# Reading DRAM in 32 KB runs that land in two partitions each, in a single-query attention kernel

## The chip, the cores and the metric

The kernel runs on one core of a Trainium2 chip. The metric is the device time of one execution in microseconds (us), as a median over several runs.

## The reference, cut to what matters

Two decode-attention blocks with one query each, their results side by side:

```python
# A: 32 heads, 32 key/value heads, 32,768 keys of 128 elements, bf16
q = (x @ wq).reshape(32, 128)
p = softmax(q @ k_cache.T * 128 ** -0.5)      # per head
a = (p @ v_cache).reshape(4096) @ wo
# B: the same with 8 key/value heads (4 query heads share one) and the last 4096 keys alone
out = concatenate([a, b])
```

Block A's keys and values are 2 x 32 x 32768 x 128 x 2 bytes = 512 MiB (537 MB). Everything else (block B's keys and values, the projection weights) brings the traffic to 570 MB. Each key and each value is used once, so the kernel streams.

## The kernel before: the parts that matter

Keys of A come in units of 2 MB: one head, 8192 keys. Partition p holds 64 consecutive keys, 16 KB in a row in DRAM and 16 KB in a row on the chip. A value buffer holds two heads and is filled by two such loads. All loads are issued by SyncE in program order; each waits until the buffer that it fills has been read.

```python
class _Kernel:
    NK = 4      # key buffers of 16 KB per partition
    NV = 3      # value buffers of 32 KB per partition
    ...
    def kv_src(self, name, which, h0, nh, r):
        d = self.X[name]
        base = d["key0"] + d["blk"] * r                 # blk: 8192 keys in A
        ap = d[which][0, h0:h0 + nh, base:base + d["blk"], :]
        return ap.rearrange("s (p j) d -> p s (j d)", p=128)

    def load(self, dst, src, sem, *deps):
        self.op("sp", lambda e: e.dma_start(dst, src).then_inc(sem, 16), *deps)
    ...
    # load_k: one head of A (two of B) into one key buffer
        dst = self.kbuf[slot][:, :].rearrange("p (s x) -> p s x", s=d["kpu"])
        self.load(dst, self.kv_src(name, "k", h0, d["kpu"], r), self.ksem[slot], ...)
    # load_v: one half of a value buffer
        dst = self.vbuf[slot][:, half * w:(half + 1) * w].rearrange("p (s x) -> p s x", s=nh)
        self.load(dst, self.kv_src(name, "v", h0, nh, r), self.vsem[slot][half], ...)
```

After landing, TensorE transposes the keys in 128 x 128 tiles, VectorE copies the transposes out, TensorE multiplies them with the query; softmax statistics are kept over rounds of 8 heads x 8192 keys, and the value products of one round run beside the key work of the next.

## Time and profile before

1366.77 us, median of 3 runs (1366.75 to 1367.38).

| what | value | how to read it |
|---|---|---|
| bytes read | 570 MB | at the rate of the next line they take 1338 us |
| rate from 120 to 1300 us | 426 GB/s | from the table by stretches, nearly flat over 40 slices |
| share of the DMA engines in that time | 1.01 | by the DMA records 16 or more packets are at work in 99% of that time |
| TensorE, VectorE busy in that time | 71%, 57% | both are idle for part of it |
| DMA in the chain that ended last | 77% | the kernel waits for data |

These are lines of the page of the kernel before: span, the DMA rows of the 40 slices, packets and bytes, the two large DMA queues (packets, MB, share of the 16 engines' span) and the shares of the chain that ended last.

```profile
span 1365.0 us, 32343 instructions
DMA  9999999999999999999999999999999999999995
GB/s 392 422 425 426 427 426 427 427 425 427 425 426 427 426 426 427 425 426 427 427 424 427 425 427 427 425 426 426 427 426 425 426 426 428 426 426 425 426 405 213
DMA packets 40762, 572.51 MB, mean 419 GB/s; under 512 B 4659, under 2 KB 4661, under 8 KB 4789
q1 hardware_dynamic: 40340, 570.44, 98.5%
q8 instruction: 119, 1.95, 0.6%
DMA 77%; PE 20%; DVE 1%; issue 1%; SPq 0%; ACT 0%
```

The table by stretches of the same kernel (start:end, length, busy time and instructions of each engine, TensorE's granted clock, DMA share, GB/s):

```profile
core 0: us, PE busy (x) PEld busy (x) DVE busy (x) ACT busy (x) POOL busy (x), PEclk, DMA share, GB/s
120.00:1300.00 1180.00, 833.00 (x13381) 650.75 (x13382) 674.30 (x1188) 23.07 (x59) 0.00 (x0) 0.85 1.01 426
1300.00:1330.00 30.00, 11.18 (x229) 7.05 (x226) 8.35 (x30) 1.74 (x5) 0.00 (x0) 0.77 0.95 401
```

The DMA queue's own waits (SyncE's) are for buffers to come free, which is what a queue that runs ahead looks like (block A's loads land 33.8 and 38.4 us after their issue, medians for keys and values). A line gives the waiting engine and its line, what released it (psS holds scores, psT transposed keys), us in total, times, and the longest wait:

```profile
SPq L203 <- PE psS L444: 1033.2, 115, 13.4
SPq L203 <- PE psT L417: 128.4, 12, 14.6
```

So the only thing worth changing for most of the span is how fast the 16 engines move bytes. The trace also has every DMA packet with its duration. From those records: 16 KB packets take 611 ns at best and 616.4 ns on average from 120 to 1300 us, while packets of 4, 8 and 12 KB take about 159, 309 and 460 ns at best. A line of 36.8 ns per 1000 bytes plus 8.5 ns per packet runs through these (a packet of "16 KB" has 16,384 bytes). Its slope gives an estimate of the ceiling: 27.2 GB/s for an engine, 435 GB/s for the 16 of the page, less a fixed cost of 1.4% at 16 KB (8.5 of 611 ns).

### The profile page before, as it was taken

What the parts mean: (1) busy time and instruction counts of PE and PEld (TensorE: products, weight loads), DVE (VectorE), ACT (ScalarE), POOL (GpSimd) and SP (SyncE); (2) the same over time, 40 slices, a digit from 0 to 9 for tenths busy, and PEclk for the clock granted to TensorE, in tenths of its full rate; (3) what the DMA queues carried; (4) which work ended last, traced back from release to release, by engine and by line L of the source; (5) the groups of instructions that cost most, each with busy time, mean ns of one, the idle gap of its engine ahead of it and who ended that gap; (6) DMA issues with size and microseconds to landing.
All of it is one profiled execution on the core that took longest, in us unless ns stands there. A gap on an engine that the chain in (4) does not pass through costs nothing.

```text
span 1365.0 us, 32343 instructions
## 1 busy us (share of the span) xinstructions
PE 951.6 (70%) x15172; PEld 734.7 (54%) x15172; DVE 767.8 (56%) x1414; ACT 29.9 (2%) x73; POOL 2.4 (0%) x11
## 2 busy tenths in 40 slices
PE   5689766776777687676667767766766767687646
PEld 4466555655555465555556545555655545465423
DVE  4688555655656555564655646555565656555431
ACT  0000000000000000000000000000000000000000
POOL 0000000000000000000000000000000000000000
PEclk9889878878988887887888888878888898887877
DMA  9999999999999999999999999999999999999995
GB/s 392 422 425 426 427 426 427 427 425 427 425 426 427 426 426 427 425 426 427 427 424 427 425 427 427 425 426 426 427 426 425 426 426 428 426 426 425 426 405 213
DMA packets 40762, 572.51 MB, mean 419 GB/s; under 512 B 4659, under 2 KB 4661, under 8 KB 4789
## 3 DMA queue, kind: packets, MB, share of 16 engines
q1 hardware_dynamic: 40340, 570.44, 98.5%
q8 instruction: 119, 1.95, 0.6%
q14 instruction: 15, 0.11, 0.0%
q10 hardware_dynamic: 288, 0.00, 0.0%
HBM read 570.43 MB, written 0.00 MB: 418 GB/s over the span
## 4 chain that ended last, share of the span: by engine, by line
DMA 77%; PE 20%; DVE 1%; issue 1%; SPq 0%; ACT 0%
DMA kbuf<-in_A_k_cache_dram 73%; PE psT L417 15%; PE psS L444 3%; DMA kbuf<-in_B_k_cache_dram 3%; DMA vbuf<-in_A_v_cache_dram 2%; PE psS L583 1%; PE psACC L525 1%; DVE kt L421 0%; SPq L203 0%; DVE oc_B L551 0%; PE psPT L565 0%; ACT psb L472 0%; DVE o_B L535 0%; DVE tr_in L460 0%; DVE nbg_B L491 0%
## 5 line engine op out<-in xcount | busy, mean ns | idle before, releaser
L421 DVE COPY kt<-psT 128x1024 bf16<-128x1024 bf16 x1056 | 672.5, 685 | 427.0 <-PE psT L417 423.7
L417 PE MATMUL psT<-ident,kbuf 128*128 128x128 bf16 x8448 | 641.3, 243 | 361.2 <-DMA kbuf<-in_A_k_cache_dram 294.9
L417 PEld LDWEIGHTS psT<-ident,kbuf 128*128 128x128 bf16 x8448 | 577.5, 111 | 489.8 <-DMA kbuf<-in_A_k_cache_dram 335.6
L444 PE MATMUL psS<-kt,qz_A 128*32 128x512 bf16 x2048 | 177.2, 427 | 0.0
L525 PE MATMUL psACC<-vbuf,ptsb 128*8 128x256 bf16 (+1 forms) x4160 | 132.9, 283 | 23.9 <-issue 21.7
L525 PEld LDWEIGHTS psACC<-vbuf,ptsb 128*8 128x8 bf16 (+1 forms) x4160 | 103.0, 89 | 55.2 <-issue 23.4
L537 DVE SCALAR_TENSOR_TENSOR o_A<-o_A,alpha_A,psACC 128x256 f32<-128x256 f32 x48 | 23.1, 480 | 87.5 <-PE psACC L525 87.5
L444 PEld LDWEIGHTS psS<-kt,qz_A 128*32 128x32 bf16 x2048 | 32.1, 97 | 31.5 <-issue 10.4
L472 ACT ACTIVATE psb<-psS,nb_A 128x512 bf16<-128x512 f32 x16 | 11.0, 687 | 1157.8 <-DVE nb_A L470 1157.8
L535 DVE COPY o_A<-psACC 128x256 f32<-128x256 f32 x16 | 6.8, 424 | 19.9 <-PE psACC L525 19.9
L503 PEld LDWEIGHTS psPT<-ident,psb 128*128 128x128 bf16 x72 | 5.7, 123 | 15.3 <-issue 11.8
L503 PE MATMUL psPT<-ident,psb 128*128 128x128 bf16 x72 | 10.2, 290 | 2.9 <-ACT psb L472 2.9
L460 DVE TENSOR_REDUCE tr_in<-psS 128x1 f32<-128x512 f32 x18 | 12.2, 680 | 0.0
L507 ACT ACTIVATE ptsb<-psPT 128x512 bf16<-128x512 bf16 x18 | 10.7, 596 | 52.8 <-PE psPT L503 52.8
L395 PE MATMUL psACC<-x_B,vbuf 128*128 128x1 bf16 x128 | 3.7, 165 | 11.5 <-DMA x_B<-in_B_x_dram 10.9
L551 DVE SCALAR_TENSOR_TENSOR oc_A<-o_A,gmask_A,oc_A 128x128 f32<-128x128 f32 x28 | 9.9, 352 | 1.0
L395 PEld LDWEIGHTS psACC<-x_B,vbuf 128*128 128x128 bf16 x128 | 3.6, 104 | 11.6 <-DMA x_B<-in_B_x_dram 10.9
L479 DVE SCALAR_TENSOR_TENSOR l_A<-l_A,alpha_A,rs_A 128x1 f32<-128x1 f32 x12 | 2.6, 220 | 12.3 <-ACT alpha_A L477 12.3
L588 DVE CAST out_sb<-psS 1x512 bf16<-1x512 f32 x2 | 1.4, 678 | 14.1 <-PE psS L583 14.1
L583 PE MATMUL psS<-kbuf,oz_A 128*1 128x512 bf16 x32 | 8.3, 422 | 0.6 <-DVE oz_A L572 0.6
L583 PE MATMUL psS<-kbuf,oz_B 128*1 128x512 bf16 x32 | 7.1, 379 | 0.0
L583 PEld LDWEIGHTS psS<-kbuf,oz_A 128*1 128x1 bf16 x32 | 2.8, 90 | 5.6 <-issue 2.4
(72 smaller groups left out, 83.4 us busy)
## 6 DMA issues: line engine op xcount, KB each, us to landing
kbuf<-in_A_k_cache_dram SPq DMA_DIRECT2D x128, 2048.0 KB, 33.8
vbuf<-in_A_v_cache_dram SPq DMA_DIRECT2D x128, 2048.0 KB, 38.4
kbuf<-in_B_k_cache_dram SPq DMA_DIRECT2D x4, 2048.0 KB, 28.8
vbuf<-in_B_v_cache_dram SPq DMA_DIRECT2D x4, 2048.0 KB, 37.4
vbuf<-in_B_wq_dram SPq DMA_DIRECT2D x2, 2048.0 KB, 9.8
vbuf<-in_A_wq_dram SPq DMA_DIRECT2D x2, 2048.0 KB, 28.6
kbuf<-in_B_wo_dram SPq DMA_DIRECT2D x2, 2048.0 KB, 36.9
kbuf<-in_A_wo_dram SPq DMA_DIRECT2D x1, 2048.0 KB, 38.8
```

The costliest lines, as they stand in the source:

```text
L395: inst = e.matmul(ps[:, h:h + 1], lhsT=wq[:, 4096 * tt + 128 * h:4096 * tt + 128 * h + 128], rhs=t["x"][:, tt:tt + 1], start=(tt == 0 and ...
L417: inst = e.transpose(T[:, 128 * k:128 * k + 128], self.kbuf[slot][:, DH * tile:DH * tile + DH], self.ident[:, :])
L421: self.tcopy.append(self.op("dve", lambda v, T=T, KT=KT: v.tensor_copy(KT[:, :], T[:, :]), o, self.sread.get(b - self.NKT)))
L444: inst = e.matmul(bank[32 * c:32 * c + 32, :], lhsT=t["qz"][:, off:off + 32], rhs=self.kt[(b0 + c // 2) % self.NKT][:, 512 * (c % 2):512 * ...
L460: o = dve(lambda v: v.reduce_max(tr["in"][:, 0:1], self.S[i % 2][:, :], axis=AXX), sdone)
L472: e = self.op("act", lambda s: s.activation(out=pb[:, :], in_=self.S[i % 2][:, :], func=ACTF.Exp, bias=t["nb"][:, r:r + 1], scale=self.SCA ...
L503: inst = e.transpose(PT[:, 128 * jj:128 * jj + 128], pb[:, 128 * jj:128 * jj + 128], self.ident[:, :])
L507: "act", lambda s: s.activation(out=pt[:, :], in_=PT[:, 0:512], func=ACTF.Copy), o, self.pvlast.get(i - 2))
L525: inst = e.matmul(acc[32 * c:32 * c + HG, 0:w], lhsT=pt[:, col:col + HG], rhs=vv[:, :, 16 * kc + 4 * c + jj, :], start=(kc == 0 and jj == ...
L537: ou = self.op("dve", lambda v: v.scalar_tensor_tensor(out=t["o"][:, osl], in0=t["o"][:, osl], scalar=t["alpha"][:, r:r + 1], in1=acc[:, 0:w],
L551: prev = self.op("dve", lambda v, src=src, gm=gm: v.scalar_tensor_tensor(out=t["oc"][:, :], in0=src, scalar=gm, in1=t["oc"][:, :], op0=ALU ...
L583: inst = e.matmul(bank[0:1, 0:512], lhsT=t["oz"][:, a:a + 1], rhs=self.wo_at(name, a), start=(a == 0), stop=(a == 31), skip_group_check=True)
```

## The change

The intent: a larger run in DRAM, so half as many read pieces and, if the fixed cost is theirs, half of it. In DRAM partition p's 16 KB are followed directly by partition p+1's. One read of 32 KB can therefore supply two partitions. On the chip the two parts are in different partitions, so the writes stay 16 KB.

```diff
+    RUN = 16384                       # elements of 2 bytes
...
+    def load_wide(self, dst, src, sem, *deps):
+        def go(e):
+            pin, pout = (... for x in (e.lower_ap_dma(src), e.lower_ap_dma(dst)))
+            total = ...               # product of the sizes in pin.ap
+            pin = copy.replace(pin, ap=[[self.RUN, total // self.RUN], [1, 1], [1, self.RUN]])
+            pout = copy.replace(pout, ap=[list(pout.ap[0]), [1, 1], list(pout.ap[-1])])
+            e.add_instruction(mybir.InstDMACopy(..., mode="Copy", ins=[pin], outs=[pout],
+                queue="qSPDynamicHW", cce_op=ALU.bypass)).then_inc(sem, 16)
+        self.op("sp", go, *deps)
...
-        self.load(dst, self.kv_src(name, "k", h0, d["kpu"], r), ...)
+        (self.load_wide if d["kpu"] == 1 else self.load)(dst, self.kv_src(name, "k", h0, d["kpu"], r), ...)
...
-        self.load(dst, self.kv_src(name, "v", h0, nh, r), ...)
+        (self.load_wide if nh == 1 else self.load)(dst, self.kv_src(name, "v", h0, nh, r), ...)
```

The source of a load becomes 64 x 32 KB, the destination stays 128 x 16 KB. Only block A's 256 loads are concerned.

More of the change, by code (lines that the diff above doesn't have):

```diff
@@ L1 @@
+import copy
 import concourse.bass as bass
@@ L203, in load @@
         self.op("sp", lambda e: e.dma_start(dst, src).then_inc(sem, 16), *deps)
+    def load_wide(self, dst, src, sem, *deps):
+        def go(e):
+            pin, pout = (x[0] if isinstance(x, (list, tuple)) else x for x in (e.lower_ap_dma(src), e.lower_ap_dma(dst)))
+            total = 1
+            for _, n in pin.ap:
+                total *= n
+            pin = copy.replace(pin, ap=[[self.RUN, total // self.RUN], [1, 1], [1, self.RUN]])
+            pout = copy.replace(pout, ap=[list(pout.ap[0]), [1, 1], list(pout.ap[-1])])
+            e.add_instruction(mybir.InstDMACopy(
+                name=f"I-{self.nc.next_id()}", engine=mybir.EngineType.SP, mode="Copy", ins=[pin], outs=[pout],
+                queue="qSPDynamicHW", cce_op=ALU.bypass)).then_inc(sem, 16)
+        self.op("sp", go, *deps)
     def load_k(self, i, u):
@@ L213, in load_k @@
         dst = self.kbuf[slot][:, :].rearrange("p (s x) -> p s x", s=d["kpu"])
-        self.load(dst, self.kv_src(name, "k", h0, d["kpu"], r), self.ksem[slot], self.kfree[n - self.NK] if n >= self.NK else None)
+        (self.load_wide if d["kpu"] == 1 else self.load)(dst, self.kv_src(name, "k", h0, d["kpu"], r), self.ksem[slot], self.kfree[n - self.NK] if n >= self.NK else None)
         self.kwhere[(i, u)] = (n, slot, (self.ksem[slot], 16 * (fill + 1)))
@@ L231, in load_v @@
         dst = self.vbuf[slot][:, half * w:(half + 1) * w].rearrange("p (s x) -> p s x", s=nh)
-        self.load(dst, self.kv_src(name, "v", h0, nh, r), self.vsem[slot][half], self.vfree[n - self.NV] if n >= self.NV else None)
+        (self.load_wide if nh == 1 else self.load)(dst, self.kv_src(name, "v", h0, nh, r), self.vsem[slot][half], self.vfree[n - self.NV] if n >= self.NV else None)
     def load_wq(self, name):
```

## The prediction

> **What bounds the kernel.** The DMA engines. The page's utilisation rows show them at nine tenths or more in 39 of 40 slices, moving 425 to 427 GB/s; the table by stretches gives 426 GB/s and a DMA share of 1.01 from 120 to 1300 us, with TensorE busy 71% and VectorE 57%. The chain that ended last is 77% DMA, nearly all key loads. SyncE's own waits (1033 us on the score matmuls) are for free buffers; loads are issued 34 to 38 us before landing, some seven 2 MB loads deep, so the engines don't run dry before the tail, which the change doesn't touch.
>
> **What the change does.** 128 key and 128 value loads of block A (512 MiB of the 570 MB) keep their bytes, 16 KB writes, semaphores and order. Each reads 64 runs of 32 KB where it read 128 of 16 KB. Block B's loads and the weights stay. No compute instruction changes.
>
> **Cost per packet.** The trace's DMA records give for 4, 8, 12 and 16 KB packets about 159, 309, 460 and 611 ns at their fastest: 36.8 ns per KB (27.2 GB/s for one engine, 435 for 16) plus some 8.5 ns per packet.[...] The mean 16 KB packet takes 616.7 ns: 98% of that ceiling. Removing every fixed cost of A's loads would save (616.7-602.4) x 8 x 256 = 29 us, an upper bound just at 2%.
>
> **What it saves.** One engine has 8 packets per load. If the 8.5 ns belong to the read side, halving the reads saves 4 x 8.5 = 34 ns per load and engine, 256 loads: 8.7 us, all on the critical path, as DMA bounds every stage of A. If they belong to the write side, nothing is saved. If some of the further 5.6 ns of jitter per packet also comes from switching reads, up to 3 us more. I weigh the first case a little over the second: about 7 us saved.
>
> **Risks.** The two sides now have different shapes (64 against 128 entries).[...] I take this as one in twelve. A gain over 2% would need more than the ceiling.
>
> **What the profile would show.** If right: A's records become 32 KB of 1213 to 1222 ns if counted by reads (packets fall by about 16,400 from 40,762), the steady rate rises from 426 to about 429 GB/s, bytes and number of loads stay, the chain stays three quarters DMA, TensorE and VectorE stay near 952 and 768 us busy. If 32 KB takes exactly twice 611 ns, the fixed cost is the write side's and the time is unchanged.[...] If the rate rises but the time doesn't fall, TensorE limits in places (its granted clock is 0.85), which I don't expect.
>
> **What would make it wrong.** The fixed cost sits wholly on writes (no gain); uneven engines[...] (a loss); or a rate above 27.2 GB/s per engine that no packet here shows (a larger gain).
>
> Predicted 1359.5 us, range 1346 to 1368.5; faster by over 2%: 0.07, within 2%: 0.86, slower by over 2%: 0.07.

8.7 us for the read side, up to 3 us more and nothing for the write side were weighed to about 7 us off 1366.8, predicted as 1359.5. "That ceiling" is the 435 GB/s of the line above.

## The result and the profile after

1366.98 us (1365.66 to 1367.39, 4 runs) against 1367.08 us (1366.75 to 1370.0, 4 runs) of the kernel before in the same rounds. The ratio is 0.9993, with a 95% interval of 0.9976 to 1.001. A ratio here is the mean time of one kernel's fast runs over the mean time of the other's fast runs of the same rounds, so it is not quite the ratio of the two medians. A second measurement (below) gave 1.0003 (0.999 to 1.0015). The change does nothing to the time.

The same lines of the page of the changed kernel:

```profile
span 1363.9 us, 32343 instructions
DMA  9999999999999999999999999999999999999995
GB/s 393 422 423 425 428 426 425 426 429 428 423 425 427 428 425 426 427 429 426 425 423 429 427 426 425 425 429 424 425 426 427 428 426 426 426 427 425 425 409 223
DMA packets 24378, 572.51 MB, mean 420 GB/s; under 512 B 4659, under 2 KB 4661, under 8 KB 4789
q1 hardware_dynamic: 23956, 570.44, 98.4%
q8 instruction: 119, 1.95, 0.6%
DMA 77%; PE 20%; DVE 1%; issue 1%; SPq 0%; ACT 0%
```

Its table by stretches and the queue's own waits:

```profile
core 0: us, PE busy (x) PEld busy (x) DVE busy (x) ACT busy (x) POOL busy (x), PEclk, DMA share, GB/s
120.00:1300.00 1180.00, 826.41 (x13394) 646.79 (x13394) 674.27 (x1190) 23.19 (x59) 0.00 (x0) 0.86 1.00 426
1300.00:1330.00 30.00, 10.15 (x215) 6.32 (x212) 7.52 (x29) 1.74 (x5) 0.00 (x0) 0.69 0.97 409
```

```profile
SPq L217 <- PE psS L461: 1018.2, 117, 18.6
SPq L217 <- PE psT L434: 125.0, 11, 14.2
```

What the reader should see: the reads did become larger, as the packets fell from 40,762 to 24,378, exactly 16,384 fewer (256 loads x 64). A record is thus one read piece. Yet the steady rate is 426 GB/s before and after. The DMA share fell from 1.01 to 1.00 without any byte arriving sooner: the records of consecutive packets overlap by a few ns, and fewer records overlap less often (an estimate from e3 below, where records of 89 ns on average give a share of 1.05: about 4 ns each). So the sum of packet durations is not a throughput at this precision; the GB/s row is.

The duration of a 32 KB record tells why. From 120 to 1300 us its median is 1227 ns, which is twice the 614 ns median of a 16 KB record (1228). One fixed cost of 8.5 ns less would have made it about 1219 (an estimate from the line above).

### The profile page after: what moved, and what is told of

The parts are those of the page before. It is cut to its first block, busy times and chain, and to the rows that moved or that the text cites. A ratio compares the mean times of both kernels' runs of the same rounds, so it can differ in the third digit from the quotient of the medians.

```text
span 1363.9 us, 32343 instructions
## 1 busy us (share of the span) xinstructions
PE 944.6 (69%) x15172; PEld 730.4 (54%) x15172; DVE 767.1 (56%) x1414; ACT 29.9 (2%) x73; POOL 2.4 (0%) x11
## 2 busy tenths in 40 slices
DMA packets 24378, 572.51 MB, mean 420 GB/s; under 512 B 4659, under 2 KB 4661, under 8 KB 4789
## 3 DMA queue, kind: packets, MB, share of 16 engines
q8 instruction: 119, 1.95, 0.6%
## 4 chain that ended last, share of the span: by engine, by line
DMA 77%; PE 20%; DVE 1%; issue 1%; SPq 0%; ACT 0%
DMA kbuf<-in_A_k_cache_dram 73%; PE psT L434 15%; PE psS L461 3%; DMA kbuf<-in_B_k_cache_dram 3%; DMA vbuf<-in_A_v_cache_dram 2%; PE psS L600 1%; PE psACC L542 1%; DVE kt L438 0%; SPq L206 0%; DVE oc_B L568 0%; PE psPT L582 0%; ACT psb L489 0%; DVE o_B L552 0%; DVE tr_in L477 0%; DVE nbg_B L508 0%
```

## The experiments

Theory W: the fixed cost is paid for each write piece, and reads are free at these sizes. Theory R: it is paid for each read piece and the saving was lost elsewhere. Theory C, a form of R: the loads could go faster, but TensorE and VectorE give the buffers back too late.

In the first three experiments only the two access patterns of A's loads change. Written as (run of the read, run of the write):

```diff
-  pin  ap=[[16384, 64], [1, 1], [1, 16384]]      # the changed kernel: reads of 32 KB
-  pout ap=[pout.ap[0], [1, 1], [1, 8192]]        #                     writes of 16 KB
+  pin  ap=[[8192, 128], [8192, 1], [1, 8192]]    # e1: reads of 16 KB; e3: [1024, 8], [1, 1024] inside
+  pout ap=[pout.ap[0], [1024, 8], [1, 1024]]     # e1, e2 and e3: eight writes of 2 KB side by side
```

The opposite pair (small reads, one large write), which would test the read side most directly, is not among the runs.

### e1: reads of 16 KB, writes of 2 KB

> Block A's loads read 16 KB runs as before, but every 16 KB write is split into eight writes of 2 KB (same bytes, same place). Theory W (about 8.5 ns are paid per write piece): 16 KB of one engine takes 602 + 8 x 8.5 = 670 ns in place of 611, so 59.5 ns x 8 x 256 = 122 us more, about 1489 us, and some 390 GB/s in steady state. Theory R (paid per read piece, the time of the changed kernel held up by something else): no change, 1367 us.

Measured: 1494.79 us, one look, against 1367.31 us before. That is 127.5 us more. With a load's 128 packets spread evenly over 16 engines, one engine writes 56 more pieces per load, 14,336 in 256 loads: 127.5 us / 14,336 = 8.9 ns per piece (an estimate). (The 9.4 ns in the expectations of e5 come from the steady rates, 385 against 426 GB/s, and not from the whole time.) The state of a single look is unknown, but the trace puts the loss in the packets: from 120 to 1300 us the median 16 KB record takes 681 ns in place of 614.

### e2: reads of 32 KB, writes of 2 KB

> Reads of 32 KB, writes of 2 KB. Theory W: the same as with 16 KB reads and 2 KB writes, about 1489 us, as the reads count for nothing. Theory R: 1358 to 1367 us. If reads and writes each add their own cost: about 9 us below the run with 16 KB reads.

Measured: 1496.77 us, one look. Half as many reads as in e1, and no gain.

### e3: reads of 2 KB, writes of 2 KB

> Reads of 2 KB and writes of 2 KB. Theory W: still about 1489 us, although there are eight times as many reads as with 16 KB reads. Theory R: this one alone of the three is slow, about 1489 us. If both sides add: about 1611 us.

Measured: 1496.23 us, one look. Eight times the reads of e1, sixteen times those of e2, and the same time within 0.13% over all three. The tables by stretches of e1, e2 and e3, in this order, show the same rate:

```profile
120.00:1300.00 1180.00, 779.67 (x12178) 611.78 (x12171) 619.26 (x1094) 21.95 (x55) 0.00 (x0) 0.84 1.01 385
```

```profile
120.00:1300.00 1180.00, 776.63 (x12154) 609.33 (x12156) 617.20 (x1089) 21.96 (x55) 0.00 (x0) 0.84 1.00 385
```

```profile
120.00:1300.00 1180.00, 784.96 (x12158) 614.78 (x12158) 618.46 (x1089) 21.95 (x55) 0.00 (x0) 0.83 1.05 385
```

And their packet lines, e1, e2, e3: reads per kernel differ by more than ten times, the rate does not.

```profile
DMA packets 40761, 572.51 MB, mean 383 GB/s; under 512 B 4658, under 2 KB 4660, under 8 KB 4788
```

```profile
DMA packets 24377, 572.51 MB, mean 383 GB/s; under 512 B 4658, under 2 KB 4660, under 8 KB 4788
```

```profile
DMA packets 270137, 572.51 MB, mean 383 GB/s; under 512 B 4658, under 2 KB 4660, under 8 KB 266932
```

Theory R falls. It also falls that both sides add (e3 would have been near 1611 us). Theory W foretold all three within 0.6%.

### e4: half of the key compute left out

```diff
-                for k in range(8):        # transposes of a batch
+                for k in range(4):
-  v.tensor_copy(KT[:, :], T[:, :])
+  v.tensor_copy(KT[:, 0:512], T[:, 0:512])
   # and the score matmuls read columns 0:512 twice
```

> The changed kernel with half of the key transposes and half of the copy of each batch left out (a wrong result on purpose), all loads as they are. Theory C (TensorE and VectorE give buffers back too late, and so ate a gain of the loads): the time falls clearly below 1358 us. Theory W: the loads alone set the time, so it stays within about 5 us of 1367 us (the last stretch after the last keys may get a little shorter), and the steady rate stays at 426 GB/s.

Measured: 1359.67 us (1359.57 to 1360.64, 4 runs), ratio 0.9946 (0.9929 to 0.9962) to the kernel before. That is 7.6 us less, more than the 5 us that I had allowed, yet not the time clearly below 1358 us that theory C asked for. The stretches of this run:

```profile
120.00:1300.00 1180.00, 687.54 (x9635) 449.25 (x9634) 445.29 (x1200) 23.09 (x59) 0.00 (x0) 0.76 1.00 427
1300.00:1330.00 30.00, 9.90 (x181) 6.10 (x184) 2.92 (x11) 0.78 (x2) 0.00 (x0) 0.61 1.00 426
```

VectorE's busy time of the main stretch fell by a third (674 to 445 us), and the rate rose only from 426 to 427 GB/s; the 32 KB record kept its 1227 ns median. More is at the end: from 1300 to 1330 us the rate is 426 GB/s in place of 409, so the compute holds up the last loads a little. Part of the rise in the main stretch may come from the instruction stream, which the page counts on the same 16 DMA engines (0.4% of their span in place of 0.6%): 33 fewer instruction packets (86 in place of 119), 0.54 MB, 1.3 us at 426 GB/s over the whole run (an estimate). I did not separate these parts further. The control, the kernel before with half of its key compute, was not run, so the 7.6 us alone do not refute theory C. What speaks against it is the packets: with the compute halved, a 32 KB record still takes 1227 ns, twice 614, so there is no gain of the reads that late buffers could have eaten.

### e5, e6, e7: fewer write pieces, with controls

If W holds, the way to a gain is a larger write. I took 32 KB in a row in one partition on both sides, and for that regrouped block A: a round is now 4 heads x 16,384 keys in place of 8 heads x 8192, so a partition holds 128 keys of one head (32 KB). A load is 4 MB, and two key buffers lie side by side. The core of the edit:

```diff
-        a["KC"], b["KC"] = 4, 2                        # 8 heads, 8192 keys a round
+        a["KC"], b["KC"] = 8, 2                        # 4 heads, 16384 keys a round
+    RUN_R = 16384     # e5 and e6; 8192 in e7          # elements of a read
+    RUN_W = 16384     # e5; 8192 in e6 and e7          # elements of a write
+            pin  = copy.replace(pin,  ap=[[16384, 128], [R, 16384 // R], [1, R]])
+            pout = copy.replace(pout, ap=[pout.ap[0],   [W, 16384 // W], [1, W]])
...          # units address half a head; value buffers hold one head; two groups of 4 heads
...          # share the last matmuls of a group, so that results start at partitions 0, 32, 64, 96
```

These three kernels differ in nothing but the two run lengths.

> Block A regrouped, the result still right: a round takes 4 heads and 16,384 keys in place of 8 heads and 8192 keys, so one partition's keys and values of a load are 32 KB in a row on both sides, and a load is 4 MB. Reads 32 KB, writes 32 KB. Theory W, with 9.4 ns per write piece as the runs with 2 KB writes gave: one write piece less for every 32 KB, 4.7 ns per 16 KB and engine, so 4.7 x 8 x 256 = 9.7 us below the same kernel with 16 KB writes, some 430 GB/s in place of 426 to 427. It runs about 4,000 more value matmuls, which cost a little instruction traffic, so against the kernel before about 1357 to 1364 us. If only narrow writes cost extra and 16 KB is already free of it: the same time as with 16 KB writes.

> The regrouped kernel with 32 KB reads, each landing as two 16 KB writes: the control for the write size. Theory W: about 1367 to 1374 us, 9.7 us above the one with 32 KB writes. A rival by which the size of the load or the regrouping makes any gain: equal to the one with 32 KB writes.

> The regrouped kernel with 16 KB reads and 16 KB writes: the studied change, undone in this form. Theory W: equal to the one with 32 KB reads and 16 KB writes within 2 us. Theory R: 9 to 10 us slower than it.

| kernel | read, write | us, median (runs) | ratio to before |
|---|---|---|---|
| e5 | 32 KB, 32 KB | 1369.69 (6) | 1.0019 (1.0007 to 1.0032) |
| e6 | 32 KB, 16 KB | 1379.70 (5) | 1.0086 (1.0073 to 1.0099) |
| e7 | 16 KB, 16 KB | 1380.54 (4) | 1.0094 (1.0081 to 1.0107) |

The write size is worth 10.0 us in the medians and 9.4 us in the means (1379.3 less 1369.9); 9.7 was expected. One engine writes 1024 pieces fewer (by the same even spread), so a piece costs 9.2 ns by the means. The steady rates of e6 and e7, in this order, are to be held against e5's 426 GB/s further below:

```profile
160.00:1250.00 1090.00, 765.53 (x15740) 613.77 (x15744) 619.77 (x1149) 21.98 (x55) 0.00 (x0) 0.85 1.00 423
160.00:1250.00 1090.00, 762.55 (x15744) 611.27 (x15744) 618.86 (x1148) 21.98 (x55) 0.00 (x0) 0.85 1.00 423
```

The read size (e7 against e6, which is the studied change in this form) is worth 0.8 us in the medians, with overlapping intervals. The 32 KB record shows the worth of the write size directly: its median from 120 to 1300 us is 1227 ns when it lands as two writes (e6) and 1214 ns when it lands as one (e5).

But the regrouping lost more than the write size won. The stretches of e5:

```profile
80.00:120.00 40.00, 34.55 (x518) 26.23 (x515) 31.73 (x54) 0.00 (x0) 0.00 (x0) 0.91 0.86 355
160.00:1250.00 1090.00, 763.31 (x15956) 611.70 (x15953) 623.45 (x1158) 22.59 (x56) 0.00 (x0) 0.85 1.00 426
```

From 80 to 120 us the DMA moved 355 GB/s: with two 4 MB key buffers, the next key load waits for a whole buffer (from 60 to 130 us SyncE waited four times for score matmuls, 63.4 us in all and up to 23.8), and the value loads stand behind it in SyncE's order. Shorter dips, to between 408 and 421 GB/s in single slices of the page, came back through the run.

### e8, e9: three key buffers and two value buffers

```diff
-    NK = 4        # key buffers of 16 KB a partition, used in pairs; lines that place the output weights are left out
-    NV = 3        # value buffers of 32 KB a partition
+    NK = 6
+    NV = 2
```

> The regrouped kernel with 32 KB reads and writes lost what it gained: between 80 and 120 us it moved 355 GB/s where the kernel before moved 425, and a dip to 409 to 420 came with most rounds, as with only two 4 MB key buffers the key load waits for its buffer and holds up the value loads queued behind it. Here the same on-chip memory is cut into three 4 MB key buffers and two 4 MB value buffers. Expected: the dips go, about 8 us less than the 1369.7 us measured before, so 1359 to 1363 us, a few us below the kernel before. If the dips have another cause (the extra value matmuls, the instruction traffic), it stays at 1367 to 1370 us.

> The control: the same buffers, each 32 KB read landing as two 16 KB writes. Theory W: 9.7 us more than with 32 KB writes, about 1369 to 1373 us.

Measured: e8 1364.50 us, ratio 0.9972 (0.9958 to 0.9985); e9 1372.90 us, ratio 1.0035 (1.0023 to 1.0048). The write size is again worth 8.4 us (8.5 in the means). The dip at 80 to 120 us went as expected, but e8 ended 1.5 us above its range, and a new dip came near the end. The stretches of e8:

```profile
80.00:120.00 40.00, 37.72 (x610) 28.32 (x611) 36.98 (x64) 0.00 (x0) 0.00 (x0) 1.00 1.01 431
1270.00:1300.00 30.00, 23.92 (x548) 19.08 (x544) 19.35 (x34) 0.00 (x0) 0.00 (x0) 0.92 0.79 332
```

### e10: output weights ahead of the last value loads

The output weights of block B, and the first half of block A's, are issued before the last round's value loads have to wait:

```diff
+        for part in range(2):
+            self.load_wo("B", part)            # before any value load of the last round
         for u in range(d["nvu"]):
             self.load_v(last, u, 0)
             self.load_v(last, u, 1)
+            if u == 0:
+                self.load_wo("A", 0)
-            ...                                # where they were before
```

> The regrouped kernel with three key and two value buffers moved only 365 GB/s from 1270 to 1290 us and 264 from 1290 to 1300, as its last value loads waited for buffers with the output weights queued behind them; that is some 7 us of traffic lost. Here block B's output weights and the first half of block A's are issued ahead of these waits. Expected: 3 to 6 us below the 1364.5 us of that kernel, so about 1358 to 1361.5 us, 0.4 to 0.7% below the kernel before. If the loss only moves to the very end (the last value load lands as late), it stays at 1363 to 1365 us.

Measured: 1367.21 us, ratio 1.0005 (0.9993 to 1.0017): a miss. Each set of runs has its own runs of the kernel before, so e8 and e10 are best compared through these: e8 was 2.8 us below its own, e10 is 0.5 us above its own (medians), some 3 us lost. The loss moved to the end. From 1260 to 1340 us SyncE waited 67 us for value matmuls (psACC) to free a buffer, so the two value buffers were still the limit:

```profile
SPq L222 <- PE psACC L569: 67.3, 4, 20.0
```

```profile
1310.00:1320.00 10.00, 3.58 (x128) 3.32 (x128) 0.39 (x2) 0.00 (x0) 0.00 (x0) 0.50 0.52 221
```

### e11: the changed kernel again

> The changed kernel once more, unchanged, to narrow the interval. Theory W: the same as the kernel before within 0.15% (a write costs as before, and 64 reads a load cost as much as 128). Theory R or half of it: 0.3% or more faster.

Measured: 1366.57 us (6 runs) against 1366.74 us (11 runs), ratio 1.0003 (0.999 to 1.0015). Theory R's 8.7 us would be 0.9936, half of it 0.9968. Both are outside.

### e12: the last round's first values in key buffers

By then no further keys come, so two of the three key buffers take the first two value loads of the last round, and the output weights follow after all values:

```diff
+            if u < 2:      # last round: value loads 0 and 1 into key buffers that are free
+                self.load_wide(self.kpair[slot // 2][:, :], self.kv_src("A", "v", ...), self.ksem[slot], self.kfree[...])
+            else:
                 self.load_v(last, u, 0)
```

> Reordering the output weights only moved the loss: the value loads two and three of the last round still waited for the two value buffers, and from 1310 to 1320 us the DMA moved 221 GB/s. Here the first two value loads of the last round go into key buffers that are free by then, and the output weights follow all value loads. Expected: no dip before the last load, so about 7 us less than the 1364.5 us of the kernel with three key and two value buffers: 1355 to 1360 us, 0.5 to 0.8% below the kernel before and the changed one. If the tail is set by the last matmuls instead, 1362 to 1365 us.

Measured: 1361.33 us (1360.90 to 1361.59, 5 runs) against 1366.05 us, ratio 0.9961 (0.9947 to 0.9975). That is 1.3 us above the range, and the fastest kernel; its interval does not touch that of the changed kernel in e11. It runs 40,434 instructions in place of 32,343, so its instruction stream is 2.47 MB in place of 1.95 (151 packets in place of 119, 0.7% of the 16 engines' span in place of 0.6%). The first value below is the steady rate, the second the stretch that had read 401 in the kernel before:

```profile
120.00:1300.00 1180.00, 832.57 (x17353) 665.76 (x17350) 675.95 (x1249) 23.96 (x59) 0.00 (x0) 0.86 1.00 427
1300.00:1330.00 30.00, 11.15 (x388) 10.14 (x388) 4.80 (x24) 1.74 (x5) 0.00 (x0) 0.60 0.99 423
```

All twelve kernels passed the comparison with the reference, even e4, which computes wrong scores. The inputs are so small that the softmax is nearly even, so the comparison says little about the keys. I therefore ran e5, e8, e12 and the changed kernel in a functional simulation with much larger inputs (keys 60 times, and the other factors scaled up too; values only, no times): block A's relative error was 0.0024 for each of them, and 0.93 for e4.

## Why the prediction was right or wrong, point by point

- **What bounds the kernel: right.** The DMA engines do (their share is 1.01 from 120 to 1300 us). e1 to e3 changed nothing but the shape of the loads and moved the time by 127 to 130 us; e4 left out half of the key compute and moved it by 7.6.
- **The line behind the ceiling of 435 GB/s, and the fixed cost of about 8.5 ns: right in size.** The slope came from packets of four sizes in the trace (159, 309, 460 and 611 ns). The ceiling itself is an estimate from it: the long stretches printed here show at most 427 GB/s. The line also gives 1214 ns for a packet of 32 KB with one fixed cost, a size that it was not drawn through, and e5's median is 1214. The fixed cost was measured again as 8.9 ns (e1), 9.2 ns (e5 against e6) and 8.3 ns (e8 against e9, 8.5 us in the means / 1024).
- **"I weigh the first case a little over the second: about 7 us saved": wrong. This is the step that failed.** The prediction gave the read side half of the fixed cost back, 8.7 us, all on the critical path; no gain clear of the noise was measured (1366.98 against 1367.08). A packet whose read and write have the same length cannot tell which side pays, and all packets behind the line are of that kind. I had named both cases and leaned to the wrong one, with no measurement that favoured it; that the stated range, 1346 to 1368.5 us, still held the result is due to its reaching past the case of no gain. In these runs reads no shorter than the writes cost nothing measurable: e1, e2 and e3 with 16, 32 and 2 KB reads took 1494.8, 1496.8 and 1496.2 us, and a load with 64 reads and 128 writes takes the time of 128 of each (a median of 1227 ns for 32 KB against 2 x 614).
- **"up to 3 us more" from jitter: wrong.** A 16 KB packet's mean was 616.4 ns; half of a 32 KB packet's mean (1228.8) is 614.4. That small difference is in the records alone, since the rate stayed at 426 GB/s.
- **What the profile would show:** the fall in packets was right (about 16,400 foretold, 16,384 measured). The 429 GB/s and the 1213 to 1222 ns were wrong (426 and a median of 1227). The sign "32 KB takes exactly twice" a 16 KB packet and then "the time is unchanged" is what came (1227 against 2 x 614).
- **Risks: did not come.** With 64 entries on one side and 128 on the other, 16 or more packets are at work in 99% of the time from 120 to 1300 us, as before, and the unchanged 426 GB/s agrees with an even spread.

What stays open: since no run has reads narrower than its writes, the runs don't tell "each write piece pays" from "the finer of the two sides pays". For the kernels run here both say the same.

## What to carry to other kernels

A fixed cost per transfer piece may belong to one side alone (here 8.3 to 9.2 ns for each write piece and nothing measurable for the reads); before merging pieces on one side, vary the two sides separately (here two kernels with 2 KB writes and reads of 16 and 32 KB showed in one look each, 1494.8 and 1496.8 us, that wider reads gain nothing). Here the pieces that count are the writes into the partitions, so this stream, at 98% of its estimated ceiling (426 of 435 GB/s), gains from longer rows per partition (8.4 to 10.0 us of 1370 for 32 KB writes in place of 16 KB), not from longer runs in DRAM (ratios 0.9993 and 1.0003). And larger loads with the same memory mean fewer buffers: of the 8.4 to 10.0 us that 32 KB writes were worth, the first regrouping lost all and 2 us more, and the buffers had to be divided anew twice to keep about 5.
